# Four row blocks for the attention weights, and a reordered start, in a fused attention and two MLP kernel

## The chip, the cores and the metric

The kernel runs on one core of one Trainium2 chip. The metric is the device time of one execution in microseconds (us). Each engine takes its instructions in order: TensorE (PE for matmuls, PEld for its weight loads), VectorE (DVE), ScalarE (ACT), GpSimd (POOL) and SyncE (SP), whose queue issues the DMAs.

## What is computed

An attention stage is followed by two MLPs, for N = 12480 tokens of 128 features, 32 inducing vectors and a hidden width of 2048:

```
def mab(q, kv):
    s = scale * (q @ kv.T)
    a = exp(s - s.max(-1)); a /= a.sum(-1) + 1e-09
    return a @ kv
h = mab(inducing, x)          # 32 x 128
x1 = mab(x, h)                # 12480 x 128
z  = x1 @ w_in                # 12480 x 2048
x2 = (max(z, 0) + alpha * min(z, 0)) @ w_out
out = max(x2 @ w2_in, 0) ** 2 @ w2_out
```

The MLP weights come as 64-bit floats and are made into 32-bit ones on the chip.

## The kernel before, in words

**Precision.** Matmuls of the MLPs run in a fast 32-bit format (fp32r). To keep accuracy each operand is split into a high part (a cast) and a low part (the rest), and a product is three matmuls: high by high, low by high, high by low (`three`, lines 645 to 648, three matmuls on lines 646, 647 and 648).

**Stages.** The first attention (lines 352 to 441) goes once over x and leaves h, transposed and repeated four times, in `hT` (line 433). The second attention (`second_attention`, line 446) is done for groups of token tiles: scores, a 32x32 block transpose, maximum and subtract (`step_max`), exponential, sum and scale (`step_sum`), transpose back. It leaves the attention weights `a_s` of a tile: 32 numbers per token, stacked in blocks of 32 rows. `a_s` of a tile holds high, low, high in three blocks (96 rows). The stationary side `w1s` holds h w_in as high, high, low in its blocks, so one matmul over 96 rows gives all three products (`l1_a`, line 636). The other user of `a_s` is line 664 in `end_y1`, against `v_s`, once per tile: it adds the term of alpha.

**Making a_s and w1s.** For the first tile (384 tokens, cut in three pieces of 128) `step_spread` copies the blocks with matmuls (line 514) and `step_split_spread` makes the parts (lines 521 and 523). For all other tiles `step_split` (line 496) makes the parts in `a_hi` and `a_lo`, and three DMAs per tile, issued by SP, put them into the blocks (line 505). For w1s, `make_w1` computes h w_in for four column blocks at once; `copy_w1` casts it on ACT into `w1s` for the first 512 columns, into `w1f` and into `w1h`; GpSimd takes the low part `w1l` (line 553); `spread_w1s` (line 555) then issues nine DMAs of 64 KB.

**Weights.** Every piece of a weight passes through a list of steps, `to_f32`: magnitude and low bits on ACT (lines 196 and 199), BITS (line 203, a shift) and SIGN (line 207, two inputs) on DVE, ADD on POOL (line 210). For w_out there follow REST (line 225, POOL), HI (line 230, ACT) and LO (line 215 through `pool_lo`, POOL). `convs[4]` to `convs[7]` are the four pieces of w_out. Their steps are put by hand between those of the attention, and program order is the order on each engine.

**Main loop.** There are 25 tiles: one of 384 tokens, three of 448 and 21 of 512; each has 16 chunks of hidden units, which makes 400 steps s. Step s issues `l1_a(s)` (one matmul of line 636, ACT line 640 for the high part, DVE line 642 for the low part `g1l`), `l2_a` of 24 steps earlier (three matmuls), then `l1_b` and `l2_b` (three matmuls each): ten matmuls a step once all are running. In the first 24 steps only line 636 and `l1_b` run, four matmuls a step, and a step's line 636 uses the PSUM bank that was freed four steps earlier by `g1l`. Extra work is hung on steps through `plan` and `at(step, function)`: the second attention of the next group, the rest of w_out, and the pieces of the second MLP's weights (`PIECES`).

**Places in memory.** Tiles of the pool `keep` lie one behind the other. `xT` has 49920 bytes per partition (195 x 256); `w1s`, `wo_hi`, `wo_lo` and the tiles of the second MLP's weights have 8192 each (32 x 256), so all of these begin at the same place modulo 256. `al` and `al1` have 64 bytes each, and so `v_s`, which follows them, lies 128 bytes off that place.

Of the kernel before, what the change touches and what calls it, by code (L numbers as in the profile page):

```python
# [9 lines left out]
F32 = mybir.dt.float32  # L10
F32R = mybir.dt.float32r
# [3 lines left out]
ALU = mybir.AluOpType  # L15
# [4 lines left out]
T = 512  # L20
# [5 lines left out]
Q = 4  # L26
# [4 lines left out]
def attention_then_two_mlps(ctx: ExitStack, tc, x, inducing, w_in, w_out, alpha, w2_in, w2_out, out):  # L31
# [3 lines left out]
    nc = tc.nc  # L35
    _, N, C = x.shape
    M = inducing.shape[0]
    DFF = w_in.shape[1]
    P = 128
    NCH = DFF // P  # L40
    wide = WIDTHS
# [12 lines left out]
    att = ctx.enter_context(tc.tile_pool(name="att", bufs=1))  # L54
# [3 lines left out]
    def bank(tag, bufs):  # L58
        return ps.tile([P, 512], F32, tag=tag, name=tag, bufs=bufs)
# [4 lines left out]
    y2_bank = lambda: bank("y2", 2)  # L64
# [4 lines left out]
    def free_bank():  # L69
        turn[0] += 1  # L70
        return ms_bank() if turn[0] % 2 or main_loop else y2_bank()

    main_loop = []

    def keep_tile(name, shape, dt=F32):
        return keep.tile(shape, dt, name=name, tag=name)

    f32 = lambda ap: ap.bitcast(F32)
# [25 lines left out]
    same = cv.tile([P, P], F32, name="same", tag="same", bufs=1)  # L104
    nc.gpsimd.memset(same, 0.0)
    for k in range(-(Q - 1), Q):
        nc.gpsimd.affine_select(
            out=same, in_=same, pattern=[[-1, P]], compare_op=ALU.not_equal, fill=1.0,
# [12 lines left out]
    def columns(v, w):  # L121
        return v if w == T else v[:, 40 : 40 + w]
# [4 lines left out]
    w1s = keep_tile("w1s", [P, DFF], F32R)  # L127
# [5 lines left out]
    x_last = keep.tile([P, DFF], F32, name="x_last", tag="w2o_hi")  # L133
    aw = keep.tile([P, NCH, P], F32, name="aw", tag="w2o_lo")
    al = keep_tile("al", [P, NCH])
    al1 = keep_tile("al1", [P, NCH])
    v_s = keep_tile("v_s", [P, P], F32R)
    hT = keep_tile("hT", [P, P])
    s_run = keep_tile("s_run", [P, 1])
# [34 lines left out]
    def load_w(name, k):  # L174
        raw = cv.tile([P, 512, 2], I32, name="raw", tag="raw", bufs=4)
        v = src[name]
        if len(v.shape) == 3:
            nc.sync.dma_start(
                out=raw.rearrange("p (c d) t -> p c (d t)", d=P), in_=v[:, 4 * k : 4 * k + 4, :]
            )  # L180
        else:
            nc.sync.dma_start(out=raw.rearrange("p c t -> p (c t)"), in_=v[:, k * 1024 : (k + 1) * 1024])
        raws[name, k] = raw
# [30 lines left out]
    def pool_lo(lo, a, hi):  # L214
        nc.gpsimd.tensor_tensor(lo, a, f32(hi), op=ALU.subtract)

    def conv_w_in(k):
        return to_f32("w_in", k, lambda: w_in_sb[:, k * 512 : (k + 1) * 512])
# [75 lines left out]
    nm, e, f, s_g, eT, hb = {}, {}, {}, {}, {}, {}  # L294
# [57 lines left out]
    convs = [conv_w_in(k) for k in range(4)] + [conv_w_out(k) for k in range(4)]  # L352
# [3 lines left out]
    b = free_bank()  # L356
    nc.tensor.transpose(b[:, :M], ind, ident[:M, :M])
    nc.vector.tensor_copy(indT, b[:, :M])
    for g in range(last):
        if g:  # L360
            run(convs[g - 1][:2])
        b = scores(g)
# [16 lines left out]
        if g == 2:  # L379
            b = y2_bank()  # L380
# [4 lines left out]
    MAG, LOW, BITS, SIGN, ADD, REST, HI, LO = range(8)  # L385

    b = scores(last)
# [6 lines left out]
    b = y2_bank()  # L394
# [9 lines left out]
    b = ms_bank()  # L404
# [1 line left out]
    keep_busy(2, idle_bank)  # L406
    add_values(last - 1)
    sums(last)
    nnm = att.tile([P, 57], F32, name="nnm", tag="nnm")[:, :1]
    nc.vector.tensor_scalar_mul(nnm, nm[last], -1.0)  # L410
    convs[5][BITS]()
    convs[5][SIGN]()
# [11 lines left out]
    d = ms_bank()  # L424
# [5 lines left out]
    b = y1_bank()  # L430
# [3 lines left out]
        hT.rearrange("c (q j) -> c q j", q=Q), b[:, :P].rearrange("c (q j) -> c q j", q=Q),  # L434
        den.unsqueeze(1).to_broadcast([P, Q, M]), op=ALU.mult,
    )
    convs[6][SIGN]()
    convs[5][REST]()
    convs[4][LO]()
    convs[6][ADD]()  # L440
    convs[6][REST]()


    a_s = {}

    def second_attention(tiles, cuts=None):

        nt = len(cuts or tiles)  # L450
        tw = wide[tiles[0]]
        n, w = nt * M, P if cuts else tw
        v = {}

        def step_scores():
            b = v["s"] = free_bank()
            for i in range(nt):
                rhs = xt_cols(tiles[0])[:, cuts[i] : cuts[i] + w] if cuts else xt_cols(tiles[i])
                nc.tensor.matmul(  # L459
                    b[i * M : (i + 1) * M, :w], hT[:, :M], rhs, start=True, stop=True,  # L460
                    tile_position=(0, i * M),
                )

        def step_transpose():
            a = v["a"] = att.tile([P, T // M, M], F32, name="a2", tag="a2")
            v["a"] = a[:n, : w // M]
            nc.vector.transpose(a[:n].rearrange("p b j -> p (b j)")[:, :w], v["s"][:n, :w])

        def step_max():
            a = v["a"]  # L470
            mx = att.tile([P, T // M], F32, name="mx", tag="mx")[:n, : w // M]
            nc.vector.reduce_max(mx, a, axis=AX.X)
            eng = nc.vector if cuts or main_loop else nc.gpsimd
            eng.tensor_tensor(a, a, mx.unsqueeze(2).to_broadcast([n, w // M, M]), op=ALU.subtract)

        def step_exp():
            nc.scalar.activation(v["a"], v["a"], AF.Exp, scale=scale)

        def step_sum():
            a = v["a"]  # L480
            sm = att.tile([P, 4 * T // M], F32, name="sm", tag="sm")[:n, : w // M]
            nc.vector.reduce_sum(sm, a, axis=AX.X)
            nc.vector.tensor_scalar_add(sm, sm, 1e-9)
            nc.vector.reciprocal(sm, sm)
            mult = nc.vector.tensor_tensor if cuts else nc.gpsimd.tensor_tensor
            mult(a, a, sm.unsqueeze(2).to_broadcast([n, w // M, M]), op=ALU.mult)

        def step_back():
            t = v["t"] = att.tile([P, T], F32, name="a2t", tag="a2t")
            nc.vector.transpose(t[:n, :w], v["a"].rearrange("p b j -> p (b j)"))  # L490

        def new_a_s(t):
            a_s[t] = columns(att.tile([P, T], F32R, name="a_s", tag="a_s", bufs=5), wide[t])[: 3 * M]
            return a_s[t]

        def step_split():

            hi = att.tile([P, T], F32R, name="a_hi", tag="a_hi")
            nc.scalar.copy(hi[:n, :w], v["t"][:n, :w])
            lo = att.tile([P, T], F32R, name="a_lo", tag="a_lo")  # L500
            pool_lo(lo[:n, :w], v["t"][:n, :w], hi[:n, :w])
            for i, t in enumerate(tiles):
                d = new_a_s(t)
                for k in range(3):
                    nc.sync.dma_start(
                        out=f32(d[k * M : (k + 1) * M]),
                        in_=f32((lo if k % 2 else hi)[i * M : (i + 1) * M, :w]),
                    )

        def step_spread():  # L510
            b = v["b"] = y1_bank()
            for i in range(nt):
                skip = max(0, cuts[i - 1] + w - cuts[i]) if i else 0
                nc.tensor.matmul(
                    b[:, cuts[i] + skip : cuts[i] + w], same_q[:n, i, :], v["t"][:n, skip:w], start=True, stop=True
                )

        def step_split_spread():

            d = new_a_s(tiles[0])  # L520
            nc.scalar.copy(d, v["b"][: 3 * M, :tw])
            lo = d[M : 2 * M]
            nc.vector.tensor_tensor(lo, v["b"][M : 2 * M, :tw], f32(lo), op=ALU.subtract)

        steps = [step_scores, step_transpose, step_max, step_exp, step_sum, step_back]
        return steps + ([step_spread, step_split_spread] if cuts else [step_split])


    w1 = {}
# [16 lines left out]
    def copy_w1():  # L546
        nc.scalar.copy(w1s[:, :512], w1["first"])
        w1["f"] = att.tile([P, 512], F32, name="w1f", tag="a_s", bufs=5)
        nc.scalar.copy(w1["f"], w1["bank"])
        w1["hi"] = att.tile([P, 512], F32R, name="w1h", tag="a_s", bufs=5)  # L550
        nc.scalar.copy(w1["hi"], w1["bank"])
        w1["lo"] = att.tile([P, 512], F32R, name="w1l", tag="a_s", bufs=5)
        pool_lo(w1["lo"], w1["f"], w1["hi"])

    def spread_w1s():
        for k in range(1, Q):
            for r, v in enumerate(("hi", "hi", "lo")):
                nc.sync.dma_start(
                    out=f32(w1s[r * M : (r + 1) * M, k * 512 : (k + 1) * 512]), in_=f32(w1[v][k * M : (k + 1) * M, :])
                )  # L560

    def step_wa():
        b = w1["wa"] = y2_bank()
# [11 lines left out]
    second = second_attention([1, 2, 3])  # L575
# [8 lines left out]
    step_wa()  # L584
    stage1.close()
    first_w1s_low()
    convs[7][BITS]()
    first[6]()
    second[0]()
    first[7]()  # L590
    convs[7][SIGN]()
    convs[6][HI]()
    load_w("w2_in", 0)
    load_w("w2_in", 1)
    load_w("w2_out", 0)
    spread_w1s()
    convs[5][LO]()
    convs[7][ADD]()
    convs[7][REST]()
    convs[6][LO]()  # L600
    load_w("w2_in", 2)


    v_bank = []

# [117 lines left out]
    def at(s, f, *a):  # L723
        plan.setdefault(s, []).append(lambda: f(*a))

    at(0, second[1])
    at(1, second[2])
    at(2, second[3])
    at(2, scale_wa)
    at(3, second[4])  # L730
    at(4, convs[7][HI])
    at(4, convs[7][LO])
    at(5, second[5])
    at(6, second[6])
    at(10, step_v)
    at(11, copy_v)
    at(14, split_v)
# [81 lines left out]
```

## Time and profile before

| | us |
|---|---|
| median of 3 runs | 975.88 (975.27 to 977.53) |
| the profiled execution | 976.8 |
| its span, first to last instruction | 975.0 |
| PE busy in the span | 960.8 |

Times below are from the start of the span. The profiled execution is 0.9 us above the median, and 1.8 us of its time lie around the span. A matmul's duration covers its whole way through the array; the array takes the next one sooner, so the time that a stream of matmuls takes is read from the starts.

### The profile page before, as it was taken

The page shows a single profiled execution, that of the slowest core. Times are in us where ns is not written, and L with a number is a line of the kernel's source. Part 1 is how long each engine was busy: PE and PEld are TensorE (multiplying, and loading weights), DVE is VectorE, ACT ScalarE, POOL GpSimd, SP SyncE. Part 2 cuts the span into 40 slices and gives each one's busy share as a digit, 9 for nine tenths or more (in the row PEclk, how much of TensorE's full clock was granted, in tenths as well). Part 3 has the DMA queues.
Part 4 walks back from the last instruction along what each step waited for, and adds up shares of the span by engine and source line. Part 5 has one row for each costly group of instructions (what it writes and reads, how often), then busy time and mean ns, then how long its engine had stood idle before and what let it go on. Part 6 is the DMA issues. An engine that isn't in the chain of part 4 may idle for free.

```text
span 975.0 us, 13667 instructions
## 1 busy us (share of the span) xinstructions
PE 960.8 (99%) x4561; PEld 792.1 (81%) x4561; DVE 659.2 (68%) x1026; ACT 728.5 (75%) x1333; POOL 535.7 (55%) x437
## 2 busy tenths in 40 slices
PE   9989999999999999999999999999999999999997
PEld 7678999887888887888887888887888887888886
DVE  5888776666766666766666666666766666766677
ACT  6678777777777777777777777777777777777775
POOL 2558665555665555565555565555565555566520
PEclk9989999999999999999999999999999999999999
DMA  9631001000010000001000001000002000001001
GB/s 324 193 96 44 9 14 29 11 10 1 12 27 17 12 2 11 11 13 32 12 1 12 11 6 39 12 1 11 11 1 43 12 1 11 11 1 19 9 4 23
DMA packets 64439, 27.32 MB, mean 28 GB/s; under 512 B 53344, under 2 KB 57968, under 8 KB 64368
## 3 DMA queue, kind: packets, MB, share of 16 engines
q1 hardware_dynamic: 63312, 26.31, 10.9%
q8 instruction: 36, 0.59, 0.3%
q14 instruction: 35, 0.29, 0.1%
q10 hardware_dynamic: 1056, 0.13, 0.1%
HBM read 14.80 MB, written 6.39 MB: 22 GB/s over the span
## 4 chain that ended last, share of the span: by engine, by line
PE 96%; DVE 2%; ACT 1%; issue 1%; POOL 0%; DVEq 0%; ACTq 0%
PE y L646 18%; PE y L647 18%; PE y L648 18%; PE h L646 9%; PE h L647 9%; PE h L636 9%; PE h L648 9%; PE h L273 1%; PE ms L287 1%; PE ms L459 1%; PE y L664 1%; PE y L337 1%; DVE g1l L642 0%; ACT g1h L640 0%; DVE mag L207 0%
## 5 line engine op out<-in xcount | busy, mean ns | idle before, releaser
L691 POOL TENSOR_TENSOR g2l<-sq,g2h 128x512 fp32r<-128x512 f32 (+2 forms) x376 | 475.5, 1265 | 353.1 <-ACT g2h L689 334.5
L642 DVE SCALAR_TENSOR_TENSOR g1l<-h,g1h 128x512 fp32r<-128x512 f32 (+2 forms) x400 | 269.7, 676 | 239.2 <-ACT g1h L640 233.1
L640 ACT ACTIVATE g1h<-h 128x512 fp32r<-128x512 f32 (+2 forms) x400 | 234.4, 588 | 152.7 <-PE h L636 150.7
L682 DVE TENSOR_TENSOR sq<-h,r 128x512 f32<-128x512 f32 (+2 forms) x400 | 270.8, 677 | 51.1 <-ACT r L680 6.6
L680 ACT ACTIVATE r<-h 128x512 f32<-128x512 f32 (+2 forms) x400 | 235.2, 588 | 64.3 <-PE h L648 59.7
L689 ACT CAST g2h<-sq 128x512 fp32r<-128x512 f32 (+2 forms) x400 | 240.4, 601 | 1.4 <-DVE sq L682 1.4
L636 PE MATMUL h<-a_s,w1s 96*128 96x512 f32 (+2 forms) x400 | 157.9, 396 | 5.5 <-DVE g1l L642 4.5
L646 PE MATMUL h<-y1h,w2i_hi 128*128 128x512 f32 (+2 forms) x400 | 157.5, 394 | 1.0 <-DVE g1l L642 1.0
L647 PE MATMUL h<-y1h,w2i_lo 128*128 128x512 f32 (+2 forms) x400 | 155.5, 389 | 0.0
L648 PE MATMUL h<-y1l,w2i_hi 128*128 128x512 f32 (+2 forms) x400 | 154.8, 387 | 0.0
L648 PE MATMUL y<-g1l,wo_hi 128*128 128x512 f32 (+2 forms) x400 | 154.5, 386 | 0.0
L647 PE MATMUL y<-g1h,wo_lo 128*128 128x512 f32 (+2 forms) x400 | 154.4, 386 | 0.0
L646 PE MATMUL y<-g1h,wo_hi 128*128 128x512 f32 (+2 forms) x400 | 154.4, 386 | 0.0
L647 PE MATMUL y<-g2h,w2o_lo 128*128 128x512 f32 (+2 forms) x400 | 153.8, 385 | 0.0
L646 PE MATMUL y<-g2h,w2o_hi 128*128 128x512 f32 (+2 forms) x400 | 153.8, 385 | 0.0
L648 PE MATMUL y<-g2l,w2o_hi 128*128 128x512 f32 (+2 forms) x400 | 153.6, 384 | 0.0
L636 PEld LDWEIGHTS h<-a_s,w1s 96*128 96x128 f32 x400 | 75.6, 189 | 26.9 <-DVE g1l L642 6.9
L646 PEld LDWEIGHTS h<-y1h,w2i_hi 128*128 128x128 f32 x400 | 75.9, 190 | 16.6 <-DVE g1l L642 1.7
L647 PEld LDWEIGHTS h<-y1h,w2i_lo 128*128 128x128 f32 x400 | 76.2, 191 | 15.5
L648 PEld LDWEIGHTS h<-y1l,w2i_hi 128*128 128x128 f32 x400 | 75.1, 188 | 16.0
L646 PEld LDWEIGHTS y<-g1h,wo_hi 128*128 128x128 f32 x400 | 75.8, 190 | 14.8
L647 PEld LDWEIGHTS y<-g1h,wo_lo 128*128 128x128 f32 x400 | 75.7, 189 | 14.5
(133 smaller groups left out, 679.1 us busy)
## 6 DMA issues: line engine op xcount, KB each, us to landing
out_dram<-o SPq DMA_DIRECT2D x82, 64.0 KB, 2.0
raw<-in_moe_w_in_dram SPq DMA_DIRECT2D x8, 512.0 KB, 5.3
xg<-in_x_dram SPq DMA_DIRECT2D x8, 512.0 KB, 9.6
raw<-in_moe_w_out_dram SPq DMA_DIRECT2D x8, 512.0 KB, 4.2
a_s<-a_hi SPq DMA_DIRECT2D x42, 64.0 KB, 2.0
a_s<-a_lo SPq DMA_DIRECT2D x21, 64.0 KB, 2.0
xg<-in_x_dram SPq DMA_DIRECT2D x4, 256.0 KB, 3.9
x_last<-in_x_dram SPq DMA_DIRECT2D x2, 512.0 KB, 10.2
```

Source lines behind the costliest of these rows:

```text
L273: nc.tensor.transpose(b[:, k * p : (k + 1) * p], x_t[g][:p, i, k, :], ident[:p, :p])
L287: nc.tensor.matmul(b[i * M : (i + 1) * M, :n], indT, xT[:, t0 : t0 + n], start=True, stop=True, tile_position=(0, i * M),)
L636: nc.tensor.matmul(b[:, :w], w1s[: a.shape[0], c * P : (c + 1) * P], a, start=True, stop=True)
L640: nc.scalar.activation(hi, b[:, :w], AF.Relu)
L642: nc.vector.scalar_tensor_tensor(lo, b[:, :w], 0.0, f32(hi), op0=ALU.max, op1=ALU.subtract)
L646: nc.tensor.matmul(b, w_hi, hi, start=start, stop=False)
L647: nc.tensor.matmul(b, w_lo, hi, start=False, stop=False)
L648: nc.tensor.matmul(b, w_hi, lo, start=False, stop=stop)
L680: nc.scalar.activation(r, b, AF.Relu)
L682: nc.vector.tensor_tensor(sq, b, r, op=ALU.mult)
L689: nc.scalar.copy(hi, sq)
L691: (nc.vector if i >= total - LAG2 else nc.gpsimd).tensor_tensor(lo, sq, f32(hi), op=ALU.subtract)
```

## The change

It does these things:

- `a_s` has four blocks of rows (high, low, high, low) for all tiles but the first: four DMAs per tile, and the matmuls of lines 636 and 664 go over 128 rows. The first tile keeps 96. The fourth product, low by low, is added to the result. `w1s` has blocks high, high, low, low: twelve DMAs in place of nine, ordered by what is made first.
- `al1` becomes 128 bytes longer, so that `v_s` begins at the same place modulo 256 as the other stationary tiles; `nnm` becomes 128 bytes longer too, so that the tiles behind it keep their place modulo 256.
- Between h and the first `a_s`: SIGN, ADD and REST of `convs[6]` are moved behind; BITS of `convs[7]` is moved ahead, to where SIGN of `convs[6]` was, and that to where BITS of `convs[7]` was. GpSimd has nothing there after LO of `convs[4]`.
- The low part of h w_in is taken by DVE from PSUM (`low_w1`), no longer by GpSimd.
- The transpose of the second group's scores is issued ahead of the main loop; its later steps are hung one step later. Its subtract goes to GpSimd. SIGN, ADD and REST of `convs[7]` go to step 1, HI and LO of `convs[6]` to step 3, those of `convs[7]` to step 5. Loads of `w2_out` 0 and `w2_in` 2 are issued later.
- Six matmuls without a reader are issued at step 3 (`keep_clock`).

```diff
-    al1 = keep_tile("al1", [P, NCH])
+    al1 = keep_tile("al1", [P, NCH + M])[:, :NCH]
...
-    nnm = att.tile([P, 57], F32, name="nnm", tag="nnm")[:, :1]
+    nnm = att.tile([P, 57 + M], F32, name="nnm", tag="nnm")[:, :1]
...
-    convs[6][SIGN]()
     convs[5][REST]()
     convs[4][LO]()
-    convs[6][ADD]()
-    convs[6][REST]()
+    convs[7][BITS]()
...
-            eng = nc.vector if cuts or main_loop else nc.gpsimd
+            eng = nc.vector if cuts or tiles[0] > 1 else nc.gpsimd
...
-            a_s[t] = columns(att.tile([P, T], F32R, name="a_s", tag="a_s", bufs=5), wide[t])[: 3 * M]
+            a_s[t] = columns(att.tile([P, T], F32R, name="a_s", tag="a_s", bufs=5), wide[t])
...
-                for k in range(3):
+                for k in range(4):
...
-            d = new_a_s(tiles[0])
+            d = a_s[tiles[0]] = new_a_s(tiles[0])[: 3 * M]
...
-        pool_lo(w1["lo"], w1["f"], w1["hi"])
-
-    def spread_w1s():
-        for k in range(1, Q):
-            for r, v in enumerate(("hi", "hi", "lo")):
...
+    def low_w1():
+        nc.vector.tensor_tensor(w1["lo"], w1["bank"], f32(w1["hi"]), op=ALU.subtract)
+
+    def spread_w1s(v, k):
+        for r in (2, 3) if v == "lo" else (0, 1):
+            nc.sync.dma_start(
+                out=f32(w1s[r * M : (r + 1) * M, k * 512 : (k + 1) * 512]), in_=f32(w1[v][k * M : (k + 1) * M, :])
+            )
...
-    convs[7][BITS]()
+    convs[6][SIGN]()
     first[6]()
     second[0]()
     first[7]()
-    convs[7][SIGN]()
-    convs[6][HI]()
+    low_w1()
     load_w("w2_in", 0)
     load_w("w2_in", 1)
+    for v, k in (("hi", 1), ("hi", 2), ("lo", 1), ("lo", 2), ("hi", 3), ("lo", 3)):
+        spread_w1s(v, k)
+    convs[6][ADD]()
+    convs[5][LO]()
+    convs[6][REST]()
+    second[1]()
     load_w("w2_out", 0)
-    spread_w1s()
-    convs[5][LO]()
-    convs[7][ADD]()
-    convs[7][REST]()
-    convs[6][LO]()
-    load_w("w2_in", 2)
+
+    def keep_clock(n):
+        b = y2_bank()
+        for _ in range(n):
+            nc.tensor.matmul(b[:, :P], same, same, start=True, stop=True)
...
-    at(0, second[1])
-    at(1, second[2])
-    at(2, second[3])
-    at(2, scale_wa)
-    at(3, second[4])
-    at(4, convs[7][HI])
-    at(4, convs[7][LO])
-    at(5, second[5])
-    at(6, second[6])
+    at(0, second[2])
+    at(1, convs[7][SIGN])
+    at(1, convs[7][ADD])
+    at(1, convs[7][REST])
+    at(1, load_w, "w2_in", 2)
+    at(3, keep_clock, 6)
+    at(3, convs[6][HI])
+    at(3, convs[6][LO])
+    at(3, second[3])
+    at(4, scale_wa)
+    at(4, second[4])
+    at(5, convs[7][HI])
+    at(5, convs[7][LO])
+    at(6, second[5])
+    at(7, second[6])
```

## Rows read from the trace of the kernel before

**Rows 1.** The page: busy time, share of the span, instructions of each engine.
```profile
PE 960.8 (99%) x4561; PEld 792.1 (81%) x4561; DVE 659.2 (68%) x1026; ACT 728.5 (75%) x1333; POOL 535.7 (55%) x437
```

**Rows 2.** Timeline of PE, one 512-token tile: start, us, engine, line, out<-in, shapes.
```profile
482.56 0.40 PE L636 MATMUL h<-a_s,w1s 96*128 96x512 f32 x1
...
519.52 0.40 PE L636 MATMUL h<-a_s,w1s 96*128 96x512 f32 x1
```

**Rows 3.** Timeline of PE near the end, where line 636 no longer runs.
```profile
947.84 0.39 PE L646 MATMUL h<-y1h,w2i_hi 128*128 128x512 f32 x1
...
951.24 0.39 PE L646 MATMUL y<-g2h,w2o_hi 128*128 128x512 f32 x1
```

**Rows 4.** Timeline of PE where tiles of 448 and of 512 mix.
```profile
186.87 0.40 PE L646 MATMUL y<-g1h,wo_hi 128*128 128x512 f32 x1
...
187.57 0.37 PE L646 MATMUL y<-g2h,w2o_hi 128*128 128x448 f32 x1
```

**Rows 5.** Timeline of DVE between h and the first a_s.
```profile
39.45 1.25 DVE L207 SCALAR_TENSOR_TENSOR mag<-raw,mag 128x512 int32<-128x512 int32 x1
...
41.28 0.71 DVE L474 TENSOR_TENSOR a<-a,mx 96x128 f32<-96x128 f32 x1
...
42.68 0.48 DVE L483 TENSOR_SCALAR sm<-sm 96x4 f32<-96x4 f32 x1
...
43.41 0.99 DVE L486 TENSOR_TENSOR a<-a,sm 96x128 f32<-96x128 f32 x1
...
45.50 1.55 DVE L203 TENSOR_SCALAR mag<-mag 128x512 int32<-128x512 int32 x1
47.08 0.55 DVE L523 TENSOR_TENSOR a_s<-y,a_s 32x384 fp32r<-32x384 f32 x1
```

**Rows 6.** Timeline of POOL, 39 to 56 us.
```profile
39.12 1.04 POOL L225 TENSOR_TENSOR aw<-w_out_sb,al 128x512 f32<-128x512 f32 x1
40.12 1.73 POOL L215 TENSOR_TENSOR wo_lo<-aw,wo_hi 128x512 fp32r<-128x512 f32 x1
41.80 1.34 POOL L210 TENSOR_TENSOR w_out_sb<-mag,raw 128x512 int32<-128x512 int32 x1
43.22 1.04 POOL L225 TENSOR_TENSOR aw<-w_out_sb,al 128x512 f32<-128x512 f32 x1
...
45.49 1.28 POOL L215 TENSOR_TENSOR wo_lo<-aw,wo_hi 128x512 fp32r<-128x512 f32 x1
...
50.80 1.27 POOL L215 TENSOR_TENSOR wo_lo<-aw,wo_hi 128x512 fp32r<-128x512 f32 x1
55.27 0.94 POOL L486 TENSOR_TENSOR a<-a,sm 96x448 f32<-96x448 f32 x1 [3.20 <-ACT g1h L640]
```

**Rows 7.** Timeline of ACT, the cast of the first a_s.
```profile
45.84 0.47 ACT L521 CAST a_s<-y 96x384 fp32r<-96x384 f32 x1 [1.55 <-PE y L514]
```

**Rows 8.** Timeline of PE, 43 to 54 us (in brackets idle time and what ended it).
```profile
43.34 0.66 PE L565 MATMUL y<-ident,w1f 128*128 128x128 f32 x4
44.90 0.91 PE L514 MATMUL y<-a2t,same_q 96*128 96x128 f32 x6 [0.90 <-DVE a2t L490]
...
47.69 0.96 PE L636 MATMUL h<-a_s,w1s 96*128 96x384 f32 x4 [1.00 <-DVE a_s L523]
```

**Rows 9.** Timeline of DVE, 50 to 59 us.
```profile
50.80 1.75 DVE L474 TENSOR_TENSOR a<-a,mx 96x448 f32<-96x448 f32 x1
...
55.04 0.95 DVE L642 SCALAR_TENSOR_TENSOR g1l<-h,g1h 128x384 fp32r<-128x384 f32 x2
...
57.90 0.56 DVE L642 SCALAR_TENSOR_TENSOR g1l<-h,g1h 128x384 fp32r<-128x384 f32 x1 [0.57 <-ACT g1h L640]
```

**Rows 10.** Sums by stretch: us, busy PE, PEld, DVE, ACT, POOL, granted clock, DMA, GB/s.
```profile
48.20:51.61 3.41, 1.86 (x8) 0.97 (x6) 3.04 (x6) 1.22 (x3) 3.10 (x3) 1.00 0.30 70
...
55.02:58.44 3.42, 3.42 (x13) 3.32 (x12) 2.60 (x6) 1.69 (x5) 3.06 (x3) 0.50 0.00 0
```

**Rows 11.** DMA issues: out<-in, queue, count, KB each, median us from issue to landing.
```profile
w1s<-w1l SPq DMA_DIRECT2D x3, 64.0 KB, 2.5
```

More of the change, by code (lines that the diff above doesn't have):

```diff
@@ L552, in copy_w1 @@
         w1["lo"] = att.tile([P, 512], F32R, name="w1l", tag="a_s", bufs=5)
-        pool_lo(w1["lo"], w1["f"], w1["hi"])
-    def spread_w1s():
-        for k in range(1, Q):
-            for r, v in enumerate(("hi", "hi", "lo")):
-                nc.sync.dma_start(
-                    out=f32(w1s[r * M : (r + 1) * M, k * 512 : (k + 1) * 512]), in_=f32(w1[v][k * M : (k + 1) * M, :])
-                )
+    def low_w1():
[5 more added lines that the diff above has]
+            )
     def step_wa():
```

## The prediction

> **What bounds the kernel now.** I read the page first: PE is busy in 960.8 of 975.0 us [rows 1], so nothing outside PE can give much, and time is won in two ways alone: PE's stream gets denser, or the stretches where PE waits get shorter. The sums by stretch put nearly all of PE's waits into the start of the main loop and the end of the first attention; later its stream has no gaps.
>
> Then the timeline of PE in the long part, by starts. A tile of 512 takes from 482.56 to 519.52 = 36.96 us [rows 2], and 161 matmuls are issued in it (16 steps of ten, and line 664), 0.2296 each. Near the end, where line 636 no longer runs, the same kinds of matmul (h from y1h, y from g2h) start 0.2267 apart: 947.84 to 951.24 is 3.40 for 15 [rows 3]. At that pace the tile would take 36.50. So 0.46 us per tile goes into something that the end of the kernel does not have. The operands of line 636 differ from the others in one thing that the code shows: 96 rows. w1s begins at the same place modulo 256 as the other stationary tiles.
>
> Then the start, engine by engine. From h (DVE ends it at about 39.5) to the first matmul of the main loop at 47.69 [rows 8] a chain runs through DVE, ACT and PE, and DVE instructions in it are long just where GpSimd is busy: a shift of line 203 took 1.55 and ended at 47.05, 0.28 after GpSimd's instruction of 45.49 [rows 5, 6]; a multiply of 96x128 took 0.99 and ended at 44.40, 0.14 after GpSimd's of 43.22; line 483 ended at 43.16, when GpSimd's of 41.80 did. DVE instructions that read SBUF alone are held until GpSimd's one is done. Later the same: the subtract took 1.75, 0.48 beyond GpSimd's of 50.80 [rows 6, 9]. After that PE's clock fell to 1.2 GHz, behind a stretch in which it was busy 1.86 of 3.41 us; granted was 0.50 still from 55.02 to 58.44, where PE was busy throughout [rows 10].
>
> **The change, part by part.**
>
> *Four row blocks.* 21 tiles of 512 times 0.46 are 9.7 us, if the excess goes with the 96 rows. Bounds: 0 (rows are not the cause) and 9.7; a loss is possible too and is a rival below. I take 9.6, near the upper end, because the end of the kernel has all the other matmuls of the step at 0.2267 [rows 3] and lacks only the one with 96 rows, and ACT and DVE read PSUM there as well. The narrower tiles I set at nothing. v_s at the other place touches 25 matmuls of 4000: inside the 0.46. Line 664, too, is in it.
>
> Here a rule speaks against it. The Trainium skill (TensorE: Matmul & The Clock Gate, LDWEIGHTS) says that a weight load takes as long for 32 rows as for 128, since its columns set the time, and its section "Why this matters for your kernels" says that one matmul of 32 rows takes the time of one of 128. By that the term is nil and the sum below 2.8; the rows have no 128-row twin of line 636 to decide it.
>
> *The DMAs.* One more per tile, three more for w1s: SP is behind by some 0.6 each, under cover of 16 steps per tile. Past the spread are moved the loads of w2_out 0 and w2_in 2, to about 51 and 52; they are first used in steps 16 and 20, over 10 us later: nothing. The low rows wait for DVE now, so the first lands at about 46.5 + 2.5 = 49.0 [rows 11]. Line 636 of chunk 4 waits for that, where its bank would be free at 47.7; but DVE has its queue until 51, so this is hidden, and without that cover costs up to 1.
>
> *h to a_s.* BITS in place of SIGN behind h: held until GpSimd's REST ends at 40.16, plus 0.28, so 40.44 and not 40.70 [rows 5, 6]: 0.26. LO of `convs[4]` then ends 1.15 behind it as before (41.85 behind 40.70), 41.59, and line 474 0.14 after that: still 0.26. GpSimd now rests. Line 483 is between 0.02 and 0.48 when not held; I take 0.2, which makes 0.54. The multiply is between 0.14 and 0.71 (line 474, held itself); I take 0.3: 1.23 in all. The spread on line 514 would come at 43.67, but PE has the transposes of line 565 until 43.34 + 0.66 = 44.00 [rows 8]; they wait for ACT, whose work is 0.26 earlier, so 43.74 in place of 44.90: 1.16. ACT ends a_s at 46.31 - 1.16 = 45.15 [rows 7]. SIGN, not held, ends at 45.50 - 1.23 + 0.7 = 44.97, so line 523 runs at 45.15 and not 47.08: **1.9 us**. Ends: 0.8 (only the held shift goes) and 2.5.
>
> *DVE's queue after a_s.* It gains `low_w1`, about 0.64 (two g1l of 384 take 0.95 [rows 9], times 512/384), and loses the subtract, 1.75. GpSimd takes that in about the 0.94 of line 486 [rows 6]. But GpSimd now has ADD, LO, REST, the subtract, ADD, REST, LO without a pause from 45 to 54, and SIGN of `convs[7]` and line 483 can each be held by one of them: 0 to 1.9, I take 1.0. Gain 0.1, ends -0.8 and 1.1.
>
> *The clock.* Six fillers run right behind the first four matmuls of the loop, at 46.5 to 48; nothing is queued there that they delay. If the clock holds, PE's 3.42 us of 55.02 to 58.44 take half [rows 10], 1.7 less; DVE, which stood idle 0.57 for a late g1h there [rows 9], limits that. Ends 0 (it falls again: PE will still wait for g1l) and 1.7; I take 0.8, the middle, near DVE's idle.
>
> *Sum.* 9.6 + 1.9 + 0.1 + 0.8 = 12.4. From the profiled execution's 976.8 that makes 964.4; it lies 0.9 above the median of the runs, by which it would be 963.5. I forecast 964.0, between the two.
>
> **The rivals.**
>
> *Rows are not the cause.* Then 2.8 remain: 973.6. For it: where tiles of 448 and 512 mix, matmuls of 128 rows are slow as well: the three y from g1h take 186.87 to 187.57, 0.233 each [rows 4]. This is also where the skill's rule would land. Against it: in pure 512 tiles the excess is there only when line 636 is. Chance 0.22.
>
> *The start gives nothing.* The clock falls in the loop again, and DVE is held at each of the two places: 1.9 - 0.8 - 0.8 (a later stretch at half clock) leaves about 0.3, and the denser stream stays: 966.5. Here keep_clock doesn't do what its name says. For it: PE waits for g1l as before. Chance 0.10.
>
> *Slower: the full-row stream runs like the mixed one.* If line 636 at 128 rows puts its neighbours out of step as in [rows 4], each of the ten matmuls takes 0.233 in place of 0.2267: 0.063 a step against 0.029 now, so 0.034 more for 336 steps, 11.4 us, less 2.8 from the start: 985. It decides from about 0.014 a step on, where it eats the start's 2.8 and 0.2% more. For it: those slow matmuls have 128 rows and the places of the fast ones. Against it: they come only with two widths. Chance 0.06.
>
> **How the numbers follow.** 0.2%, about 2 us, is what a measurement of this kernel can tell from none. Forecast 0.60, faster. Rows not the cause, 0.22: with a start worth -0.8 to 5.3 by the ends above, mostly faster (0.14), else the same (0.08). Start lost 0.10, faster. Slower rival 0.06. The last 0.02: neither part works, the same. Together 0.84 faster, 0.10 the same, 0.06 slower. The range goes down to 960.8 (the start at its upper ends, 2.5 + 1.1 + 1.7, with the whole of the stream's term) and up to 974.0, to hold the first rival's time; the slower rival and a start that gives nothing without the stream lie outside.
>
> **What would show it.** Right: a 512 tile, start to start, near 36.5; line 636 with 128*128 and starts 0.227 apart; first matmul of the loop at about 45.8; lines 483, 486 short; no held DVE instruction between h and a_s; granted clock 1.00 between 50 and 60. Wrong: a tile still at 36.96 (rows were not it) or above; line 523 still behind a long DVE instruction; long SIGN or line 483 after a_s, with PE waits on g1l as long as before; chunk 4 waiting for a DMA of w1s.

## The result and the profile after

The changed kernel takes 965.59 us (median, 964.59 to 965.83), beside 976.38 (975.27 to 977.53) for the kernel before: a ratio of 0.9887, 95% interval 0.987 to 0.9905, 10.8 us less. The forecast was 964.0 with a range of 960.8 to 974.0. The profiled execution spans 963.8 us, 11.2 less than before. In the changed kernel line 636 is line 639, 642 is 645, 664 is 667, and the lines of the second attention (459 to 523) have moved up by two.

The page's line on busy time, which answers to [rows 1]: PE is still the bound.

```profile
PE 952.1 (99%) x4573; PEld 789.9 (82%) x4573; DVE 656.6 (68%) x1026; ACT 728.0 (76%) x1333; POOL 534.1 (55%) x437
```

The timeline of PE over 16 steps of 512 tokens, line 667 among them, as in [rows 2]:

```profile
477.14 0.39 PE L639 MATMUL h<-a_s,w1s 128*128 128x512 f32 x1
...
513.64 0.39 PE L639 MATMUL h<-a_s,w1s 128*128 128x512 f32 x1
```

161 matmuls in 36.50 us, 0.2267 apart, the pace of [rows 3]. The tile gives 0.46 us. By the first line that reads w1s in each step, the changed kernel is 1.91 us ahead at step 24 and still 1.92 ahead at step 40; from there it grows with the tiles, to 11.2 at the end. So 1.9 come from the start and 9.3 from the stream.

The start. DVE from h to the first `a_s`, answering to [rows 5]:

```profile
39.31 0.99 DVE L203 TENSOR_SCALAR mag<-mag 128x512 int32<-128x512 int32 x1
...
40.87 0.70 DVE L472 TENSOR_TENSOR a<-a,mx 96x128 f32<-96x128 f32 x1
...
42.26 0.17 DVE L481 TENSOR_SCALAR sm<-sm 96x4 f32<-96x4 f32 x1
...
42.67 0.29 DVE L484 TENSOR_TENSOR a<-a,sm 96x128 f32<-96x128 f32 x1
...
44.06 0.69 DVE L207 SCALAR_TENSOR_TENSOR mag<-raw,mag 128x512 int32<-128x512 int32 x1
44.90 0.55 DVE L521 TENSOR_TENSOR a_s<-y,a_s 32x384 fp32r<-32x384 f32 x1
```

Lines 481 and 484 (483 and 486 before) fell from 0.48 and 0.99 to 0.17 and 0.29, while GpSimd had nothing to do. These are GpSimd's instructions in that time, answering to [rows 6]; between the two it stands still for 3.46 us, until SIGN on DVE and the first `a_s` are made:

```profile
39.97 1.45 POOL L215 TENSOR_TENSOR wo_lo<-aw,wo_hi 128x512 fp32r<-128x512 f32 x1
44.88 1.28 POOL L210 TENSOR_TENSOR w_out_sb<-mag,raw 128x512 int32<-128x512 int32 x1 [3.46 <-ACT a_s L519]
```

Not every DVE instruction that reads SBUF alone is held. In the kernel before, three others ran beside GpSimd's instructions of 41.80, 43.22 and 44.22; the timeline of DVE:

```profile
42.37 0.28 DVE L482 TENSOR_REDUCE sm<-a 96x4 f32<-96x128 f32 x1 [0.38 <-ACT a L477]
...
43.20 0.17 DVE L484 RECIPROCAL sm<-sm 96x4 f32<-96x4 f32 x1
...
44.44 0.31 DVE L490 STREAM_TRANSPOSE a2t<-a 96x128 f32<-96x128 f32 x1
```

They took 0.28, 0.17 and 0.31 in the changed kernel too, where GpSimd rested. The held ones have two inputs in SBUF, or are of the kind TENSOR_SCALAR.

PE from the spread to the tenth matmul of line 639 in the loop, answering to [rows 8] (matmuls of the loop are counted by line 639, 636 before, from here on):

```profile
43.50 0.85 PE L512 MATMUL y<-a2t,same_q 96*128 96x128 f32 x6
...
45.50 1.17 PE L639 MATMUL h<-a_s,w1s 96*128 96x384 f32 x4 [0.27 <-DVE a_s L521]
46.51 1.50 PE L605 MATMUL y<-same 128*128 128x128 f32 x12
...
54.15 0.44 PE L639 MATMUL h<-a_s,w1s 96*128 96x384 f32 x1 [1.77 <-DVE g1l L645]
```

The loop starts 2.19 us earlier. The fillers (line 605) run, but PE waits 1.77 us later on (1.80 before), and the sums by stretch show that the clock falls again. It is at half for 3.41 us; before, it was at half from 51.61 to 58.44, the second part of which is in [rows 10]. The first part before, then two stretches of the changed kernel:

```profile
51.61:55.02 3.41, 1.95 (x6) 1.95 (x7) 3.34 (x7) 2.44 (x6) 0.46 (x1) 0.50 0.60 168
```

```profile
51.07:54.48 3.41, 1.40 (x7) 0.99 (x7) 3.34 (x7) 1.44 (x4) 2.92 (x3) 1.00 0.42 96
54.48:57.89 3.41, 3.41 (x32) 2.89 (x34) 1.71 (x4) 2.42 (x6) 2.67 (x3) 0.50 0.72 267
```

PE was busy 1.40 of the 3.41 us before the fall. What it waited for, there and behind, stands on three engines, DVE, POOL and ACT in that order:

```profile
52.49 0.92 DVE L481 TENSOR_SCALAR sm<-sm 96x14 f32<-96x14 f32 x1
53.44 0.24 DVE L482 RECIPROCAL sm<-sm 96x14 f32<-96x14 f32 x1
53.60 0.95 DVE L645 SCALAR_TENSOR_TENSOR g1l<-h,g1h 128x384 fp32r<-128x384 f32 x2
54.80 0.64 DVE L488 STREAM_TRANSPOSE a2t<-a 96x448 f32<-96x448 f32 x1 [0.25 <-POOL a L484]
```

```profile
52.11 1.26 POOL L215 TENSOR_TENSOR wo_lo<-aw,wo_hi 128x512 fp32r<-128x512 f32 x1
53.82 0.94 POOL L484 TENSOR_TENSOR a<-a,sm 96x448 f32<-96x448 f32 x1 [0.45 <-DVE sm L482]
```

```profile
55.47 0.56 ACT L497 CAST a_hi<-a2t 96x448 fp32r<-96x448 f32 x1 [1.90 <-DVE a2t L488]
```

Line 481 is held until GpSimd's instruction of 52.11 ends. Behind it on DVE comes the low part of chunk 5 (first of the two at 53.60), for which PE waits the 1.77; and behind it come the scale on GpSimd, the transpose back, and ACT's `a_hi`, for which ACT stands 1.90 us with the next high parts queued behind it. This chain is new in no part: in the kernel before the same steps stood one step earlier.

### The profile page after: what moved, and what is told of

Same layout as the page of the kernel before. It is cut to its first block, busy times and chain, and to the rows that moved or that the text cites. A ratio compares the mean times of both kernels' runs of the same rounds, so it can differ in the third digit from the quotient of the medians.

```text
span 963.8 us, 13715 instructions
## 1 busy us (share of the span) xinstructions
PE 952.1 (99%) x4573; PEld 789.9 (82%) x4573; DVE 656.6 (68%) x1026; ACT 728.0 (76%) x1333; POOL 534.1 (55%) x437
## 4 chain that ended last, share of the span: by engine, by line
PE 96%; DVE 1%; ACT 1%; POOL 1%; issue 1%; DVEq 0%; ACTq 0%
PE y L650 18%; PE y L649 18%; PE y L651 18%; PE h L649 9%; PE h L651 9%; PE h L650 9%; PE h L639 9%; PE h L273 1%; PE ms L287 1%; PE ms L457 1%; PE y L337 1%; PE y L667 1%; DVE g1l L645 0%; ACT g1h L643 0%; PE h L95 0%
## 5 line engine op out<-in xcount | busy, mean ns | idle before, releaser
L639 PE MATMUL h<-a_s,w1s 128*128 128x512 f32 (+2 forms) x400 | 155.4, 390 | 4.2 <-DVE g1l L645 3.8
L649 PE MATMUL h<-y1h,w2i_hi 128*128 128x512 f32 (+2 forms) x400 | 154.4, 386 | 1.0 <-DVE g1l L645 1.0
L639 PEld LDWEIGHTS h<-a_s,w1s 128*128 128x128 f32 (+1 forms) x400 | 75.0, 188 | 25.8 <-DVE g1l L645 6.7
L650 PEld LDWEIGHTS y<-g2h,w2o_lo 128*128 128x128 f32 x400 | 75.1, 188 | 14.7
L649 PEld LDWEIGHTS y<-g2h,w2o_hi 128*128 128x128 f32 x400 | 75.1, 188 | 14.6
L651 PEld LDWEIGHTS y<-g1l,wo_hi 128*128 128x128 f32 x400 | 75.4, 188 | 13.9
```

Source lines behind the costliest of these rows:

```text
L639: nc.tensor.matmul(b[:, :w], w1s[: a.shape[0], c * P : (c + 1) * P], a, start=True, stop=True)
L649: nc.tensor.matmul(b, w_hi, hi, start=start, stop=False)
L650: nc.tensor.matmul(b, w_lo, hi, start=False, stop=False)
L651: nc.tensor.matmul(b, w_hi, lo, start=False, stop=stop)
```

## The experiments

The theory after the result was the forecast's: the stream's part belongs to the 96 rows, the start's part to GpSimd's rest. A point needed for all readings of the start: h itself comes at another time in each execution (38.7 to 39.8 us in these profiles), so what follows `a_s` is measured from the first matmul of the loop. Behind the 19th all kernels but the 64-row one run alike (the 26th comes 8.15 to 8.20 us later). The 19th comes 18.73 us behind the first before the change and 19.02 after it:

```profile
66.42 0.47 PE L636 MATMUL h<-a_s,w1s 96*128 96x448 f32 x1 [0.77 <-DVE g1l L642]
```

```profile
64.52 0.48 PE L639 MATMUL h<-a_s,w1s 128*128 128x448 f32 x1 [0.79 <-DVE g1l L645]
```

**Rows back (e1).**

```diff
-            a_s[t] = columns(att.tile([P, T], F32R, name="a_s", tag="a_s", bufs=5), wide[t])
+            a_s[t] = columns(att.tile([P, T], F32R, name="a_s", tag="a_s", bufs=5), wide[t])[: 3 * M]
...
-                for k in range(4):
+                for k in range(3):
```

> The changed kernel with a_s cut back to 96 rows (three DMAs per tile, matmuls against the first 96 rows of w1s and v_s); v_s stays at its new place and the start stays as changed. Theory (the excess belongs to the 96-row matmul): a 512 tile takes 36.9 us again, from start to start, in place of 36.5, and the time goes up by about 9 us, to 974 to 975. Rival (the place of v_s, or the reordered start, made the stream denser): a tile stays at 36.5 and the time at 965 to 966.

Measured: 974.53 us (973.89 to 974.82), ratio to before 0.9985 (0.9976 to 0.9995). The timeline of PE over the same 16 steps:

```profile
473.63 0.40 PE L639 MATMUL h<-a_s,w1s 96*128 96x512 f32 x1
...
510.58 0.40 PE L639 MATMUL h<-a_s,w1s 96*128 96x512 f32 x1
```

36.95 us again, with the start as changed. All but 0.4 us of the stream's part goes with the rows: this kernel is 1.98 ahead of the one before at step 40 and 2.36 at the end. By the trace's starts, in 512-token tiles, the excess lies on the 96-row matmul and the three behind it: the next one starts 0.233, 0.237, 0.233 and 0.231 after them (medians), and 0.227 with 128 rows.

**Rows alone (e2).** The kernel before with the four lines that make four blocks:

```diff
-            a_s[t] = columns(att.tile([P, T], F32R, name="a_s", tag="a_s", bufs=5), wide[t])[: 3 * M]
+            a_s[t] = columns(att.tile([P, T], F32R, name="a_s", tag="a_s", bufs=5), wide[t])
...
-                for k in range(3):
+                for k in range(4):
...
-            d = new_a_s(tiles[0])
+            d = a_s[tiles[0]] = new_a_s(tiles[0])[: 3 * M]
...
-            for r, v in enumerate(("hi", "hi", "lo")):
+            for r, v in enumerate(("hi", "hi", "lo", "lo")):
```

> The kernel before with four row blocks alone (four DMAs per tile, twelve for w1s); v_s stays at its old place, nothing of the start is reordered. Theory: a 512 tile takes 36.5 us, and the time falls by about 9 us, to 966 to 967.5; first matmul of the main loop still at 47.7. Rival (rows and the place of v_s are both needed): part of the 9 us stays away, 968 or more, with slow starts around the matmul with v_s or in every step.

Measured: 967.38 us (966.86 to 968.55), ratio 0.9914 (0.99 to 0.9929), 8.7 us less than before. The same view:

```profile
478.90 0.39 PE L636 MATMUL h<-a_s,w1s 128*128 128x512 f32 x1
...
515.40 0.39 PE L636 MATMUL h<-a_s,w1s 128*128 128x512 f32 x1
```

36.50. Rows alone give nearly all of the stream's part; e1 and e2 leave 1.5 to 1.8 us for the rest of the change. The start tells something on the clock as well: it was at half from 47.69 to 57.93, 3.4 us longer than before, and the 19th matmul came 18.60 behind the first, no later than in the kernel before.

**The place of v_s (e3).**

```diff
-    al1 = keep_tile("al1", [P, NCH + M])[:, :NCH]
+    al1 = keep_tile("al1", [P, NCH])
...
-    nnm = att.tile([P, 57 + M], F32, name="nnm", tag="nnm")[:, :1]
+    nnm = att.tile([P, 57], F32, name="nnm", tag="nnm")[:, :1]
```

> The changed kernel with the two tiles al1 and nnm at their old lengths, so that v_s lies 128 bytes off the place of the other weights again. Theory: only 25 matmuls have v_s, so at most 0.5 us more: 965.6 to 966.1, starts around it at 0.232 at worst. Rival (the place matters for the whole stream, because a slow matmul puts those behind it out of step): over 2 us more, a tile above 36.6.

Measured: 966.4 us (965.44 to 966.67), ratio 0.9904 (0.9887 to 0.992). The median is 0.8 above the changed kernel's and 0.3 above the range expected, but the two were not measured side by side and their ranges overlap: the time alone doesn't settle it. The matmuls with v_s do: minimum, median and maximum of their durations in ns, changed kernel and then e3.

```profile
L667 PE MATMUL y<-a_s,v_s x25: 340/389/397, 67.0 to 926.4; 128*128 128x512 f32 x21, 128*128 128x448 f32 x3, 96*128 96x384 f32 x1
```

```profile
L667 PE MATMUL y<-a_s,v_s x25: 336/397/397, 66.5 to 926.3; 128*128 128x512 f32 x21, 128*128 128x448 f32 x3, 96*128 96x384 f32 x1
```

At the old place the median is 397 in place of 389, with 128 rows in both: moving the stationary tile by 128 bytes has an effect of its own. (That 256 bytes are the period is not shown: one shift was tried.) By the trace's starts, the matmul before it and this one begin 0.233 and 0.234 before the next, in place of 0.227, and a tile takes 0.014 us more, 0.3 us for all. Matmuls in other steps are untouched.

**No fillers (e4).**

```diff
-    at(3, keep_clock, 6)
```

> The changed kernel without the six fillers of step 3. Theory: the fillers keep the clock for one stretch longer; without them it falls a stretch of 3.4 us earlier, as in the kernel before, and the time is 0.5 to 1.5 us longer. Rival (the fillers do nothing, since PE waits for DVE in that stretch at either clock): within 0.3 us of 965.6 with the 11th matmul of the loop at the same place.

Measured: 965.73 us (965.06 to 966.15), ratio 0.9895 (0.9881 to 0.991): the rival by the time. The clock fell at 49.1 us and was back at 52.5; PE was busy all that time, and its wait behind it shrank from 1.77 to 1.10. So from the first to the 19th matmul it took 18.63 us, less than the changed kernel's 19.02. (The 11th came at 9.45 in place of 9.83, so not at the same place: with fillers the half clock fell on it.)

**More fillers (e5).**

```diff
+    at(8, keep_clock, 8)
```

> The changed kernel with eight more fillers behind step 8, where PE waits 1.8 us for the low part of chunk 5. Theory (after a_s the start is bound by the chain sum, scale, transpose back, cast on DVE, POOL and ACT, not by PE's clock): the clock stays at 1.00 from 50 to 60, the 12th matmul of the loop comes earlier, but the 18th at most 0.5 us earlier; time 965.0 to 965.8. Rival (the clock bounds that stretch): 1.5 us or more less, 964 or below.

Measured: 965.44 us (965.3 to 965.56), ratio 0.989 (0.9875 to 0.9904). Sums by stretch:

```profile
51.07:54.48 3.41, 3.16 (x23) 2.71 (x22) 3.34 (x7) 1.62 (x4) 2.89 (x4) 1.00 0.41 84
54.48:57.89 3.41, 3.41 (x45) 2.71 (x45) 1.90 (x4) 2.23 (x5) 2.86 (x3) 1.00 0.82 299
```

PE busy 3.16 of 3.41 us before, granted clock 1.00 after. The 12th matmul comes 11.26 us behind the first in place of 12.79, but the 19th 18.63 in place of 19.02, and it does so within 0.01 in e3, where the clock happened to stay up with no more fillers. The 19th in e5:

```profile
64.32 0.47 PE L639 MATMUL h<-a_s,w1s 128*128 128x448 f32 x1 [0.66 <-DVE g1l L645]
```

A clock that holds is worth 0.4 us here, beside an execution in which it falls over these matmuls. What PE wins it waits at the 13th to 15th matmul, each of which begins 0.06 after a low part (of chunks 8 to 10) whose high part stood behind `a_hi` on ACT.

**64 rows (e6).** The low parts of h w_in and of v are left out of the product for all tiles but the first.

```diff
-                d = new_a_s(t)
-                for k in range(4):
+                d = a_s[t] = new_a_s(t)[: 2 * M]
+                for k in range(2):
```

> The changed kernel with two row blocks (64 rows) for all tiles but the first: the low parts of h w_in and of v are left out of the product. It tells whether the excess goes with the missing rows or is particular to 96. If it goes with the missing rows: the excess is double, 0.9 us per 512 tile, a tile near 37.4. If any number of rows below 128 puts the stream out of step alike: 36.9 to 37.0. If only 96 does it: 36.5.

Measured: 1121.71 us, a single run. None of the three expectations was near. The timeline of PE over a step:

```profile
565.54 0.50 PE L639 MATMUL h<-a_s,w1s 64*128 64x512 f32 x1
565.97 0.50 PE L649 MATMUL h<-y1h,w2i_hi 128*128 128x512 f32 x1
566.30 0.39 PE L650 MATMUL h<-y1h,w2i_lo 128*128 128x512 f32 x1
...
567.89 0.39 PE L651 MATMUL y<-g2l,w2o_hi 128*128 128x512 f32 x1
568.21 0.50 PE L639 MATMUL h<-a_s,w1s 64*128 64x512 f32 x1
```

The step takes 2.67 us, not 2.27: the matmul before starts 0.32 ahead, the 64-row one 0.43, the next 0.33, in place of three times 0.227. That is 0.40 us for each 64-row matmul, against 0.027 for a 96-row one (0.46 for the 17 of a tile): neither more missing rows at the same price nor a matter of 96 alone. That another mechanism is at work is likely, not shown. The Trainium skill (TensorEngine Tiling (Array Packing), Key Properties) says that a change of the tiling mode drains the engine; its section Available Configurations lists a mode of 64 rows and none of 96. The 0.40 would fit that, though no run here shows that the 64-row matmul ran in such a mode; the 0.027 is not explained by it.

**GpSimd busy again (e7).** The order before for `convs[6]` and `convs[7]` BITS:

```diff
+    convs[6][SIGN]()
     convs[5][REST]()
     convs[4][LO]()
-    convs[7][BITS]()
+    convs[6][ADD]()
+    convs[6][REST]()
...
-    convs[6][SIGN]()
+    convs[7][BITS]()
...
-    convs[6][ADD]()
     convs[5][LO]()
-    convs[6][REST]()
```

> The changed kernel with SIGN, ADD and REST of convs 6 back between h and a_s, and BITS of convs 7 back behind the first tile's low part. Theory (DVE instructions that read SBUF alone are held by GpSimd): lines 481 and 484 take 0.5 and 1.0 again, line 203 before a_s over 1.4, the first matmul of the loop comes 1.3 to 2 us later than 45.5, and the whole of that stays: 966.8 to 967.6. Rival (it is hidden in the wait for the chain after a_s): first matmul later, but under 0.5 us on the whole.

Measured: 966.45 us (966.41 to 966.72), ratio 0.9901 (0.9884 to 0.9917), 1.0 more than e5 and 0.9 more than the changed kernel, a little below the range expected. DVE's timeline (lines 483 and 486 are 481 and 484 of the changed kernel), then GpSimd's and PE's:

```profile
42.52 0.48 DVE L483 TENSOR_SCALAR sm<-sm 96x4 f32<-96x4 f32 x1
...
43.24 1.00 DVE L486 TENSOR_TENSOR a<-a,sm 96x128 f32<-96x128 f32 x1
...
45.34 0.43 DVE L203 TENSOR_SCALAR mag<-mag 128x512 int32<-128x512 int32 x1
```

```profile
44.20 1.26 POOL L215 TENSOR_TENSOR wo_lo<-aw,wo_hi 128x512 fp32r<-128x512 f32 x1
```

```profile
46.78 1.17 PE L639 MATMUL h<-a_s,w1s 96*128 96x384 f32 x4 [0.27 <-DVE a_s L523]
```

The holds on the scale are back as in [rows 5], and the loop starts at 46.78, 1.28 later. The shift before `a_s` is not held, other than expected. In [rows 6] LO of `convs[5]` held it, from 45.49; here that LO runs at 44.20 and ends 0.1 after the shift begins. It stood behind the low part of w1 on GpSimd before (1.31 us, from 44.22), and that is on DVE in this kernel. So the shift's part belongs to `low_w1`, not to the order. The profiled spans differ by 0.8 and not by 1.28, since here the clock stayed up in the loop: 18.49 from the first to the 19th.

**The subtract back on DVE (e8).**

```diff
-            eng = nc.vector if cuts or tiles[0] > 1 else nc.gpsimd
+            eng = nc.vector
```

> The changed kernel with the second group's subtract back on DVE. By my prediction DVE's queue has the subtract's time to lose and gains holds, so that little is left: within 0.5 us of 965.6. Rival (moving the subtract off DVE is what pays in the start): the subtract takes 1.0 to 1.8 on DVE, the low parts of chunks 2 and 3 come 1 to 2 us later, and the time is 1 us or more longer.

Measured: 965.33 us (964.98 to 965.82), ratio 0.9889 (0.9874 to 0.9904). The subtract took 1.17 us on DVE, and from the first to the 19th matmul it was 18.93, beside 18.63 of e5, both with the clock up: moving it is worth 0.3 us, too little for the times to show.

**LO later (e9).**

```diff
-    at(3, convs[6][LO])
...
+    at(5, convs[6][LO])
     at(5, convs[7][HI])
```

> The changed kernel with LO of convs 6 on GpSimd moved from step 3 to step 5, so that it no longer holds line 481 (0.92 in place of 0.17) and the scale behind it. Theory (the chain sum, scale, transpose back, cast bounds the start after a_s): line 481 takes 0.2, a_hi comes 0.7 earlier, and so does the 18th matmul of the loop: 964.6 to 965.2. Rival (ACT's queue alone bounds it, or the clock): within 0.2 us of the changed kernel.

Measured: 964.91 us (964.52 to 965.26), ratio 0.9884 (0.9869 to 0.9898). DVE, then ACT and PE:

```profile
53.22 0.17 DVE L481 TENSOR_SCALAR sm<-sm 96x14 f32<-96x14 f32 x1
...
54.77 0.64 DVE L488 STREAM_TRANSPOSE a2t<-a 96x448 f32<-96x448 f32 x1 [0.24 <-POOL a L484]
```

```profile
55.45 0.56 ACT L497 CAST a_hi<-a2t 96x448 fp32r<-96x448 f32 x1 [1.16 <-DVE a2t L488]
```

```profile
64.11 0.47 PE L639 MATMUL h<-a_s,w1s 128*128 128x448 f32 x1 [0.67 <-DVE g1l L645]
```

Line 481 takes 0.17 in place of 0.92, ACT's wait shrinks by 0.74, and the 19th matmul (last line) comes 17.89 behind the first, 0.74 less than in e5; the clock stayed up in both. So the hold on line 481 costs one for one. It delays two things alike, the low part of chunk 5 right behind it on DVE (8.59 to 7.85 behind the first matmul) and `a_hi`; which of them carries it to the 19th this run doesn't tell.

**Transpose back and split later (e10).** As e9, and

```diff
-    at(6, second[5])
-    at(7, second[6])
+    at(8, second[5])
+    at(9, second[6])
```

> As the run before, and the transpose back and the split of the second group hung two steps later (8 and 9 in place of 6 and 7), so that ACT does not stand for 1.9 us before a_hi with three high parts behind it. Theory: ACT and DVE go on with the chunks meanwhile, the 12th matmul comes 1.5 us or more earlier and the 18th 1 to 2 us earlier: 963.6 to 964.6. Rival (the first 512 hidden units of the next tile then wait for the DMAs of its a_s, which start later): PE waits for a_s at the 17th matmul, and the gain is gone.

Measured: 964.28 us (964.18 to 964.54), ratio 0.9877 (0.986 to 0.9893). ACT and then PE:

```profile
54.35 0.50 ACT L643 ACTIVATE g1h<-h 128x384 fp32r<-128x384 f32 x1
...
56.02 0.57 ACT L497 CAST a_hi<-a2t 96x448 fp32r<-96x448 f32 x1 [0.24 <-DVE a2t L488]
```

```profile
61.47 0.45 PE L639 MATMUL h<-a_s,w1s 128*128 128x448 f32 x1 [0.35 <-DMA a_s<-a_lo]
...
63.16 0.47 PE L639 MATMUL h<-a_s,w1s 128*128 128x448 f32 x1
```

ACT stands 0.24 for `a_hi`; the 19th matmul is 17.33 behind the first, 0.56 less than in e9. The time is as expected, but not by the way expected: the 12th matmul comes no earlier (10.50 behind the first, 10.53 in e9) and the 18th 0.11 later. The 13th to 15th gain, since the low part of chunk 8 is done 9.61 behind the first matmul in place of 11.36: this part goes with `a_hi` on ACT. At the 17th the rival comes true, PE waits 0.35 for the DMA of the next tile's `a_s` and the gain is gone. What is left comes at the 19th, which waited 0.67 for a low part in e9 and waits for none here.

**HI and LO of the last piece later (e11), beside the changed kernel (e12).** As e10, and

```diff
-    at(5, convs[7][HI])
-    at(5, convs[7][LO])
+    at(7, convs[7][HI])
+    at(7, convs[7][LO])
```

> As e10, and HI and LO of convs 7 hung at step 7 in place of 5, so that ACT does not stand 1.06 us for GpSimd's REST before that HI with a high part behind it. Theory (the start is a set of in-order waits on ACT and DVE for GpSimd): low parts of chunks 5 and 6 come 0.5 to 1 us earlier; 963.5 to 964.3. Rival (DVE's sum and scale are the bound by now): 964.1 to 964.5, as e10.

> The changed kernel once more, unaltered, beside e11 on the same chip. 965.0 to 966.0; where the clock falls in the start can differ from the first run, which should be worth no more than 0.5 us.

Measured on one chip: e11 963.89 us (963.54 to 964.07), ratio 0.987 (0.9854 to 0.9887); the changed kernel again 965.44 (964.9 to 966.19), ratio 0.9888 (0.9873 to 0.9903). From the first to the 19th matmul e11 takes 17.32, e10 17.33: the last move gives nothing, although its time lies in the theory's range. The low parts of chunks 5 and 6 end where they did (7.84 and 8.30 behind the first matmul in both), right behind the sum and the scale's steps on DVE, as the rival has it. e11 is 1.55 us faster than the changed kernel on the same chip, and the runs of the two don't overlap. Not all of that is the moves' own: the clock fell in e12's profiled execution (19.01 to the 19th) and stayed up in e11's; against e5, with the clock up (18.63), the moves give 1.3. e11 is the fastest kernel tried.

## Why the prediction was right

**Four row blocks** (9.6 forecast): right in mechanism and size. The tile went from 36.96 to 36.50, as the pace at the end of the kernel had said; 9.3 us of the span, 8.9 by the times of e1 and the changed kernel, 8.7 by e2. What was known only by leaving the suspect out (the end of the kernel) is shown by putting it back (e1) and by taking it alone (e2). Most of the 0.3 that is missing is in the choice of tiles: where 448 and 512 columns mix (steps 72 to 96) nothing is gained, 0.7 less than forecast, and the tiles of 448, set at nothing, gave 0.2 (the lead goes from 1.92 at step 40 to 2.15 at step 64). v_s was right as "inside the 0.46": 0.014 per tile (e3).

The rule of the Trainium skill (TensorE: Matmul & The Clock Gate, LDWEIGHTS) agrees with the trace in what it names: the weight load takes 188 to 189 ns with 96 rows and with 128. What its section "Why this matters for your kernels" says of one matmul doesn't carry over to this stream, where a 96-row matmul costs 0.027 on itself and those behind it; the measurement decides, and the rival "rows are not the cause" fell.

**The slower rival.** Its evidence [rows 4] had another cause: with 128 rows everywhere, the mixed stretch is as slow as before. The timeline of PE:

```profile
186.83 0.39 PE L649 MATMUL y<-g1h,wo_hi 128*128 128x512 f32 x1
...
187.53 0.37 PE L649 MATMUL y<-g2h,w2o_hi 128*128 128x448 f32 x1
```

Three matmuls of 512 in 0.70 us, 0.233 each. That goes with the mix of tiles, not with rows. The operands of 448 columns differ in place too (they begin 160 bytes further in), so whether it is the width isn't shown.

**The DMAs**: as said. The first low rows of w1s were issued at 46.20 and landed at 48.15; chunk 4 began at 48.28, after 0.27 us of idle time. The view puts that down to a low part, but chunk 0's had ended at 47.16, so it was the DMA. It is hidden: ACT came to chunk 4 only at 50.28, behind the exponential.

**h to a_s** (1.9 forecast): from h's own start the loop begins 6.40 us later in place of 8.45, 2.05 less. Lines 481 and 484 gave 0.31 and 0.70 (0.28 and 0.69 forecast). e7 puts 1.28 of it down to the order around GpSimd; the rest, 0.77, is put down to `low_w1`, which let LO of `convs[5]` end before the shift; this is read from the trace and was not tried alone. The rule it rested on, that DVE instructions which read SBUF alone are held until GpSimd's is done, is too wide: lines 482, 484 and 490 were not held (0.28, 0.17 and 0.31 with GpSimd busy or at rest). The sum used it only for kinds that were held.

**DVE's queue** (gain 0.1 forecast): by DVE's own instructions as forecast. Both holds came, 0.2 on SIGN (0.88) and 0.75 on line 481 (0.92), and with `low_w1` (0.69) they ate the subtract's 1.75, whose own worth e8 shows as 0.3. The two terms of DVE and the clock can't be told apart in the time: together they were forecast at 0.9, and gave 0.1 where the clock stayed up (18.63 in e5, beside 18.73 before, where it was at half for 6.83 us).

**The clock** (0.8 forecast): this step failed. "If the clock holds" did not come true; it fell again, for one stretch, and cost 0.4 against executions where it stayed. And where it held (e3, e5) the loop took 18.63, which leaves it nothing beside DVE's 0.1. The term was sized from PE's busy time at half clock, on the ground that PE was busy throughout; but PE's work was not what bounded the stretch up to the 19th matmul. In e2 it was at half 3.4 us longer than before at no cost. The bound was the hold on line 481 with what stands behind it on DVE and, through the transpose back, on ACT (e9: 0.74 taken out of it came out at the 19th matmul in full; e10). The note that DVE's idle time would limit the gain pointed that way and was not followed to ACT, which stood 1.7 to 1.9 us for `a_hi`.

**The signs and the second rival.** Of the signs named for being right, two did not come: the clock was not at 1.00 from 50 to 60, and DVE was held behind h (line 203 took 0.99, as the forecast's own sum has it). Of those for being wrong, the long SIGN and line 481, a PE wait as long as before (1.77 beside 1.80) and chunk 4's wait for a DMA came. Both conditions of the rival "the start gives nothing" came true, then, and the start gave 1.9 all the same: the rival had the holds and the clock at 0.8 each, and they left the two terms of DVE and the clock at -0.3 together. One slip bears on the chances alone: the lower end of the start is given as -0.8, and the three ends it is made of (0.8, -0.8, 0) make 0.0.

The sum was 12.4 and came out as 11.2 in the span: 0.3 less in the stream, 1.2 less from the clock (a cost of 0.4 in place of a gain of 0.8), 0.15 more from h to a_s, and 0.14 since h itself came that much earlier in this execution. The 0.14 is luck: without it and the unforeseen 0.15 the time would lie 0.3 further from the forecast.

## What to carry to other kernels

Read a stream's pace from the starts, and find a stretch of the same kernel that lacks one suspect: 0.006 us or so on four of a step's ten matmuls was 9 us here, and no wait, no idle time and no busy share showed it. Here a matmul of 96 or 64 rows was not free of cost among matmuls of 128; try it padded to 128 rows before calling its rows saved work. Where an in-order engine has a step of a side chain between the main loop's instructions, hang that step after its inputs are there: ask what stands behind it, and whether a GpSimd instruction holds the DVE step ahead of it. And price a slow clock by what bounds the stretch, not by the engine's busy time.

## What the runs showed that was not expected

- A 64-row matmul between 128-row ones cost 0.40 us (e6: 2.67 us per step in place of 2.27), fifteen times what a 96-row one costs. Leaving the low parts out of the product made the kernel 156 us slower.
- Moving a stationary tile by 128 bytes changes the spacing of its matmul and the one ahead (0.234 and 0.233 for 0.227), with nothing else changed in the main loop (e3).
- Keeping TensorE's clock up by fillers was worth 0.4 us at most, and nothing where they stood (e4, e5).
- DVE's reductions, reciprocals and block transposes ran beside GpSimd without being held (0.28, 0.17 and 0.31 us in both kernels); the additions and shifts by a scalar and the instructions with two inputs in SBUF were held.
- Why 96 rows put the matmuls behind out of step at all stays open. Other widths were not tried by themselves; in the stretch of 448 columns before, the three matmuls behind line 636 were 0.203, 0.202 and 0.201 apart from the next (medians), and 0.200 after, so the price there is some quarter of the 0.027.
